# Block 0's first two feature rows as twenty-four parts by pair of heads, two tiles in a PSUM bank, with a new layout of the front stage

## The chip, the cores and the metric

The kernel runs on one core of a Trainium2 chip. The metric is the device time of one execution in microseconds (us), as the median of several runs.

## The reference

Three parts follow each other: an attention with a near and a far part, a dense layer with three candidates per hidden feature, and a layer of eight experts of which each token takes one. Only the first two matter here.

```python
# q, k, v: (4 batches, 8 heads, 576 positions, 64); factor 4
q_d = q.reshape(B, H, Sd, 4, D).mean(axis=3)        # k_d, v_d alike
far  = np.repeat(softmax(q_d @ k_d.T / 8) @ v_d, 4, axis=2)
mask = np.abs(pos[:, None] - pos[None, :]) < 4
near = softmax(np.where(mask, q @ k.T / 8, -1e9)) @ v
x = (far + near).transpose(0, 2, 1, 3).reshape(2304, 512)
h = np.maximum(np.maximum(x @ w1, x @ w2), x @ w3)  # (2304, 768)
x = h @ w_out                                       # (2304, 512)
# then: gate = argmax(x @ w_gate); out = p_gate * (relu(x @ w1[e]) @ w2[e])
```

## The kernel before, in words

**The attention's units.** The attention is cut into 16 units, one for each of the 4 batches and each of the 4 pairs of heads. Unit u is batch u // 4, pair u % 4. A unit loads its q and k transposed (tiles `qt`, `kt`) and its v (`vr`, `vb`), multiplies the near scores (`ts`, L408), takes maximum, exponential and sum (`smx`, `sm`, `sms`), turns the result on TensorE (`tt`) and multiplies it with v (`to`, L578); the far part does the same on rows summed by fours (`qk`, `td`, `dmx`, `ds`, `tu`, `tz`). At the end the two are added (`x`, L587), and x is split into a high half and a low half in the reduced fp32 format that TensorE takes (`xb`, L627 and L629). The low half is what the program calls `xl0` and `xl1`, one for each half of the positions.

**Forms.** The same piece can be done in several ways. The table `FORMS` gives each unit a set of two-letter flags: `pp` sums q and k by fours on TensorE (`tp`, L373) instead of VectorE; without `pb` and `px` the sum of far and near is made on VectorE; `pb` lets TensorE multiply the far part at full length (L564), `px` adds the far part on TensorE (L597); `nn` and `fn` put the normalisations on GpSimd; `nb`, `np` choose how the near maximum is subtracted, `np` on TensorE (L432).

**The weights.** w1, w2, w3 come as 64-bit floating-point words. Each of 18 pieces (6 columns blocks m times 3 matrices g) is loaded (`raw`, L816), its sign is cleared on ScalarE (L782), four VectorE operations of 128x512 narrow it to fp32 (L789, L791, L795, L799), ScalarE rounds it to a high half (`wh`, L804), and the low half `wl` is the rest: by a subtraction on VectorE or GpSimd (L807), or by two matmuls on TensorE (`wlow`, L843 and L844) with a copy behind them. The table `LOW` says which engine.

**The blocks.** x has 2304 rows (tokens), which are multiplied in nine blocks of 256. For each block 18 tiles of 128 features x 256 tokens are made, three (g = 0, 1, 2) for each of six **feature rows** m. A tile is 12 matmuls into one PSUM bank: four pairs of heads kk times three terms (high·high, high·low, low·high), all in `mul` (L1267), TensorE's row `hp<-xb,wh` and `hp<-xb,wl`. The three tiles of a feature row are reduced by a copy on ScalarE (`hid_first`, L1274) and two maxima on VectorE (`hid_max`, L1277), and later multiplied by w_out. There are four banks for this (`mm`).

**The order.** Nothing of this is placed by hand. A list scheduler, `Plan`, holds for each engine the time up to which it is filled. Each piece of work has an engine, an estimated duration, pieces that must come before it, buffers that it takes and gives back, and a due time `want`; the planner takes one after another and so fixes the order of instructions on each engine, including the order in which SyncE issues loads. The due times come from tables (`BATCH`, `PAIR`, `STEP`, `WEIGHTS`, `W_OUT`, `HIDDEN`, `ROWS`). Where TensorE would be idle by the plan for long, the planner puts in **fills**: matmuls of a constant that nobody reads (`warm`, L2401). On the chip each instruction waits for what it needs, in this fixed order.

Before, block j could begin when the low halves of **all** units of the batches it touches were done, `us = [4 * b + i ...]` in the last loop of the listing.

Of the kernel before, what the change touches and what calls it, by code (L numbers as in the profile page):

```python
# [19 lines left out]
B, H, S, D = 4, 8, 576, 64  # L20
# [11 lines left out]
TB = 256  # L32
# [18 lines left out]
FORMS = (  # L51
    "dv fn pb pp px sk sq",
    "nb nn np pb px sk sq",
    "dv fn nn np px sq xl xp",
    "pp sk xl",
    "nn pb px xl xp",
    "fn nn pp px sq xl",
    "nb px sq xl xp",
    "dv fn pp px xl xp",
    "dv nb np sk",  # L60
    "nb np sk xl",
    "dv nn sk sq xp",
    "nb sk",
    "nb np pp sq",
    "dv sk sq xp",
    "dv fn nn xl xp",
    "fn nb nn np sk xl xp",
)

LOW = (  # L70
    "DVE", "Pool", "DVE", "Pool", "DVE", "DVE",
    "PE", "Pool", "Pool", "Pool", "DVE", "Pool",
    "DVE", "DVE", "PE", "PE", "DVE", "DVE",
    "DVE", "Pool", "Pool", "DVE", "PE", "Pool",
)


BATCH, PAIR, STEP = (-278.0, 574.2, -146.8, 833.4), 90.18, (45.2, 112.5, 182.1, -110.2, -78.0, -138.8, 70.2, -165.1, -443.7, 7.1)
WEIGHTS, W_OUT = (-143.0, -97.3, 241.0, 361.9, 306.7, 570.1), (-2456.29, 74.04)
HIDDEN, ROWS, RESTS = (772.13, 191.47, -1093.51), (-324.96, -1170.55), 10.0  # L80

# [208 lines left out]
class Attention:  # L290
# [331 lines left out]
    def to_x(s, u, g, lo, on):  # L622
        xf = s.st[u]["x", g].rearrange("p a r -> p (a r)") if ("x", g) in s.st[u] else s.st[u]["to", g]
        for j, c, f, n in s.cut(u, g):
# [3 lines left out]
            else:  # L628
                s.on(on).tensor_tensor(out=w[:, 1], in0=xf[:, f:f + n], in1=w[:, 0].bitcast(F32), op=ALU.subtract)  # L629

    def plan(s, pl, u, want, flags):

        here, T = {}, STEP
# [5 lines left out]
        def add(name, eng, dur, fn, *after, t=0.0, get=(), put=(), act=None):  # L639
            after = [here[a] if isinstance(a, str) else a for a in after]  # L640
            port = eng == "Pool" or eng == "DVE" and name not in free and name not in ("sq", "sk")
            here[name] = pl.add(eng, dur, fn, after, want + t, get, put, act, port=port)
# [59 lines left out]
        if not one:  # L702
            add("of", "PE", 0.8, lambda: s.out_far(u), "cf", "sv", t=T[7], get=("at", "dn"), put=("pd", "vr"),
                act=0.54)
            add("cd", "ACT", 0.19, lambda: s.mean_far(u), "of", t=T[7], put=("at",))
        if one:
            for g in range(2):
# [3 lines left out]
                    act=1.09,  # L711
# [37 lines left out]
class Dense:  # L749
# [183 lines left out]
    def plan_block(s, pl, j, x, when):  # L933
# [8 lines left out]
        top, low, seven = {}, {}, j in SEVEN  # L942
        s.hid[j] = [None] * 6
        for n, m in enumerate((0, 1, 2, 4, 3, 5) if seven else range(6)):
            w = when(j) + n * 3
            for g in range(3):
                after = [pe, *x] if not m + g else [pe]
                after.append(s.jw[3 * m + g])

                def mul(m=m, g=g):  # L950
                    if m + g == 0:
                        first()
                    s.mul(j, m, g)

                pe = pl.add(
                    "PE", 1.37, mul, after, w, get=("mm",) if m + g else ("mm", s.ht_tag(j)),
                    put=("xb",) if m + g == 7 else (),
                )
                s.read[3 * m + g] = pe
                if g == 0:  # L960
                    b = pl.add("ACT", 0.27, lambda m=m: s.hid_first(j, m), [pe], w + HIDDEN[2], get=("hf",),
                        put=("mm",))
                else:
                    b = pl.add("DVE", 0.34, lambda m=m, g=g: s.hid_max(j, m, g), [pe, b], w + HIDDEN[2], put=("mm",), port=False)
            top[m], r = b, None
# [1406 lines left out]
def moe_kernel(ctx, tc, q, k, v, vs, w1, w2, w3, w_out, w_gate, e1, e2, cst, out):  # L2372
# [11 lines left out]
    with tc.manual_schedule():  # L2384
# [148 lines left out]
```

## Time and profile before

| what | value |
|---|---|
| median of 3 runs | 685.31 us (683.45 to 685.78) |
| the profiled execution: time, span, granted clock | 684.8 us, 683.0 us, 0.998 |
| TensorE busy (share of the span) | 667.1 us (98%) |
| VectorE busy | 432.0 us (63%) |
| ScalarE busy | 312.6 us |
| GpSimd busy | 127.0 us |
| first matmul of block 0 | 76.49 us after the span's start |

The span is the time from the first to the last instruction in the profile. The execution's own time is 1.8 us more than the span and 0.5 us below the median of the three runs. Busy time of TensorE counts the fills, which produce nothing. Busy shares are averages over stages that are limited by different things, so the stretch ahead of block 0 (the first 76.49 us) and the stretch behind it have to be read apart.

### The profile page before, as it was taken

What the parts mean: (1) busy time and instruction counts of PE and PEld (TensorE: products, weight loads), DVE (VectorE), ACT (ScalarE), POOL (GpSimd) and SP (SyncE); (2) the same over time, 40 slices, a digit from 0 to 9 for tenths busy, and PEclk for the clock granted to TensorE, in tenths of its full rate; (3) what the DMA queues carried; (4) which work ended last, traced back from release to release, by engine and by line L of the source; (5) the groups of instructions that cost most, each with busy time, mean ns of one, the idle gap of its engine ahead of it and who ended that gap; (6) DMA issues with size and microseconds to landing.
All of it is one profiled execution on the core that took longest, in us unless ns stands there. A gap on an engine that the chain in (4) does not pass through costs nothing.

```text
span 683.0 us, 16157 instructions
## 1 busy us (share of the span) xinstructions
PE 667.1 (98%) x6329; PEld 603.8 (88%) x6329; DVE 432.0 (63%) x1089; ACT 312.6 (46%) x904; POOL 127.0 (19%) x148
## 2 busy tenths in 40 slices
PE   8889999999999999999999999999999999999995
PEld 5566799989999999999999999998998989886775
DVE  5998986795544483225845558778653554597863
ACT  3765656676444353213322223441543443447753
POOL 2535432302401020101000000303211112101011
PEclk9999999999999999999999999999999999999999
DMA  7757524334422110101000005401617453463620
GB/s 250 236 171 233 193 69 117 117 92 149 127 76 59 57 40 1 50 1 49 1 32 1 33 1 182 173 33 32 189 48 241 138 174 102 138 208 126 231 83 31
DMA packets 32246, 73.18 MB, mean 107 GB/s; under 512 B 4319, under 2 KB 4575, under 8 KB 32160
## 3 DMA queue, kind: packets, MB, share of 16 engines
q1 hardware_dynamic: 26528, 57.63, 26.5%
q0 software_dynamic: 3040, 9.70, 4.3%
q10 hardware_dynamic: 2592, 4.72, 1.8%
q8 instruction: 52, 0.85, 0.5%
q14 instruction: 34, 0.28, 0.1%
HBM read 75.18 MB, written 9.70 MB: 124 GB/s over the span
## 4 chain that ended last, share of the span: by engine, by line
PE 88%; DVE 8%; DMA 1%; issue 1%; ACT 0%; SPq 0%; POOL 0%; POOLq 0%; DVEq 0%; ACTq 0%
PE hp L1267 32%; PE ehp L2043 11%; PE yp L1302 7%; PE eo L2015 7%; PE yp L1176 3%; PE ehp L2169 3%; PE eo L2210 3%; PE eo L2070 3%; PE racc L2332 2%; PE tp L373 2%; PE to L578 1%; PE ts L408 1%; PE xtp L2154 1%; PE tz L550 1%; PE tt L523 1%; PE td L489 1%
## 5 line engine op out<-in xcount | busy, mean ns | idle before, releaser
L1267 PE MATMUL hp<-xb,wh 128*128 128x256 f32 x1296 | 231.5, 282 | 0.3 <-issue 0.3
L1267 PEld LDWEIGHTS hp<-xb,wh 128*128 128x128 f32 x1296 | 196.4, 188 | 2.3 <-issue 1.4
L1267 PE MATMUL hp<-xb,wl 128*128 128x256 f32 x648 | 180.1, 278 | 0.0
L1267 PEld LDWEIGHTS hp<-xb,wl 128*128 128x128 f32 x648 | 121.9, 188 | 0.0
L1277 DVE TENSOR_TENSOR hf<-hf,hp 128x256 f32<-128x256 f32 x108 | 45.3, 420 | 74.9 <-PE hp L1267 73.3
L2043 PEld LDWEIGHTS ehp<-xT,ew 128*128 128x128 f32 x672 | 78.2, 188 | 4.2 <-issue 2.5
L2043 PE MATMUL ehp<-xT,ew 128*128 128x256 f32 x672 | 80.6, 279 | 0.0
L1284 ACT CAST ht<-hf 128x256 fp32r<-128x256 f32 (+1 forms) x54 | 21.1, 391 | 75.6 <-DVE hf L1277 75.3
L2139 POOL DMA_INDIRECT xg<-y,r_go x14 | 15.4, 1103 | 173.2 <-DMA eh<-in_moe_w_dram 112.0
L2227 POOL DMA_INDIRECT out_dram<-ob,r_si x17 | 17.2, 1014 | 117.7 <-ACT ob L2222 56.9
L1274 ACT COPY hf<-hp 128x256 f32<-128x256 f32 x54 | 20.2, 373 | 36.3 <-PE hp L1267 36.1
L2015 PE MATMUL eo<-eh,ehT 128*128 128x256 f32 x210 | 36.4, 280 | 0.0
L2015 PEld LDWEIGHTS eo<-eh,ehT 128*128 128x128 f32 x210 | 30.6, 188 | 2.5 <-issue 1.7
L2015 PE MATMUL eo<-el,ehT 128*128 128x256 f32 x130 | 31.4, 276 | 0.0
L2036 DVE SCALAR_TENSOR_TENSOR ob<-eo,r_ga,ob 128x256 f32<-128x256 f32 (+1 forms) x15 | 8.6, 571 | 32.4 <-PE eo L2015 31.6
L1966 ACT ACTIVATE ehT<-ehp 128x128 fp32r<-128x128 f32 (+1 forms) x40 | 13.3, 332 | 33.6 <-PE ehp L2043 32.7
L1288 DVE TENSOR_TENSOR ht<-hf,ht 128x256 fp32r<-128x256 f32 (+1 forms) x54 | 21.7, 402 | 10.0 <-ACT ht L1284 9.5
L1302 PE MATMUL yp<-wob,ht 128*128 128x264 f32 (+1 forms) x216 | 27.8, 284 | 0.0
L1302 PEld LDWEIGHTS yp<-wob,ht 128*128 128x128 f32 x216 | 26.7, 188 | 0.1
L1302 PE MATMUL yp<-woa,ht 128*128 128x256 f32 x216 | 26.1, 277 | 0.0
L1968 DVE SCALAR_TENSOR_TENSOR ehT<-ehp,ehT 128x128 fp32r<-128x128 f32 (+1 forms) x40 | 14.2, 354 | 18.4 <-ACT el L1951 16.5
L508 ACT ACTIVATE ds<-td,dmx 72x144 f32<-72x144 f32 x64 | 23.5, 376 | 4.9 <-DVE dmx L502 4.9
(333 smaller groups left out, 1389.5 us busy)
## 6 DMA issues: line engine op xcount, KB each, us to landing
rw<-in_moe_w_dram SPq DMA_DIRECT2D x64, 256.0 KB
eh<-in_moe_w_dram SPq DMA_DIRECT2D x20, 512.0 KB
el<-in_moe_w_dram SPq DMA_DIRECT2D x20, 512.0 KB
raw<-in_moe_w_dram SPq DMA_DIRECT2D x18, 512.0 KB
vb<-in_vs_dram SPq DMA_DIRECT2D x16, 320.0 KB
qt<-in_q_dram SPq DMA_DIRECT2D x16, 288.0 KB
kt<-in_k_dram SPq DMA_DIRECT2D x16, 288.0 KB
vr<-in_v_dram SPq DMA_DIRECT2D x16, 288.0 KB
```

What stands on the lines that cost most here:

```text
L508: s.nc.scalar.activation(out=st["ds"][:, a, :, h], in_=t[:, a].rearrange("p (k t) -> p t k", t=3), func=ACTF.Exp, bias=st["dm"][:, h, a:a ...
L1176: s.nc.tensor.matmul(s.yb[j, k][:, 0:n], h[x], r[y], start=first and i + p == 0, stop=i == 2 and p == 2, skip_group_check=True,)
L1267: s.nc.tensor.matmul(t, s.part(a, m, g)[:, kk], s.xb[j][:, x, kk], start=n == 0, stop=n == 11)
L1277: s.nc.vector.tensor_tensor(out=s.hf[j, m], in0=s.hf[j, m], in1=s.hp.pop((j, m, g)), op=ALU.max)
L1284: s.nc.scalar.copy(out=s.ht[j][:, 0, m, c], in_=s.hf[j, m][:, c])
L1288: s.nc.vector.tensor_tensor(out=s.first_low(j) if j in SEVEN and not m else h[:, 1, m, c], in0=s.hf[j, m][:, c], in1=h[:, 0, m, c].bitcast ...
L1302: s.nc.tensor.matmul(b[j, t, g], s.ht[j][:, int(i == 1), kk, ts], s.wo(int(i == 2), kk, g)[:, 0:n], start=q == 0, stop=q == 17)
L2015: s.nc.tensor.matmul(t, x[:, c:c + 128], y, start=m == 0 and first, stop=m == 11, skip_group_check=True,)
L2043: s.nc.tensor.matmul(t, s.W1[j][a][:, f * 128:(f + 1) * 128], s.xL[:, x, j], start=n == 0, stop=n == 11,)
L2070: s.nc.tensor.matmul(s.op[k, 0], h[a][:, j, i * 128:(i + 1) * 128], s.second(b, j), start=j == 0 and w == 0, stop=j == 7 and w == 2,)
L2169: s.nc.tensor.matmul(s.hp[k][f], a[:, j], s.W1[j][b][:, f * 512:(f + 1) * 512], start=j == 0 and w == 0, stop=j == 3 and w == 2,)
L2210: s.nc.tensor.matmul(s.op[k, cols.start], a[:, j], s.second(b, j, cols), start=j == 0 and w == 0, stop=j == 7 and w == 2)
```

## The change

Four things change together.

1. For block 0 the first six tiles (feature rows m = 0 and 1) are no longer made one after another. `plan_parts` makes 24 **parts** of three matmuls, ordered by pair of heads kk: six tiles for kk = 0, then six for kk = 1, and so on. A part waits for x of its own pair of heads and for its own weight. Two tiles share one bank of 2x256 columns, so the six hold three of the four banks from the first part until both tiles of a bank have been read; only the first matmul into a bank clears it. For kk = 3 the two tiles of a bank change places (`i ^= kk == 3`). For m = 1 the first copy is made by VectorE instead of ScalarE.
2. A block waits only for those low halves whose positions fall into it. For block 0 these are the first halves `xl0` of units 0 to 3.
3. The planner gets extra edges (`BEHIND`): the near and the far scores of unit u may be held back until the output multiplication `on` of unit u - v is placed.
4. All tables are new: the forms, the engine of each low half, one due time per unit instead of `BATCH` and `PAIR`, and the due times of weights and blocks.

```diff
 FORMS = (
-    "dv fn pb pp px sk sq",
+    "dv fn pp px sk sq xl",
...
 LOW = (
-    "DVE", "Pool", "DVE", "Pool", "DVE", "DVE",
+    "PE", "PE", "PE", "Pool", "Pool", "DVE",
...
+PARTS, PART = 6, 2219.9
...
-        add("n", "PE", 1.05, lambda: s.near(u), "lq", "lk", s.masked, get=("at", "at", "sm"), act=1.3)
+        add("n", "PE", 1.05, lambda: s.near(u), "lq", "lk", s.masked, s.behind(u, 0), get=("at", "at", "sm"), act=1.3)
...
+        parts, free = s.plan_parts(pl, x, when(j), first) if not j else [], []
...
-                pe = pl.add(
-                    "PE", 1.37, mul, after, w, get=("mm",) if m + g else ("mm", s.ht_tag(j)),
-                    put=("xb",) if m + g == 7 else (),
-                )
-                s.read[3 * m + g] = pe
+                if n * 3 + g < PARTS and not j:
+                    pe = parts[n * 3 + g & ~1]
...
+                e, d, x1 = ("ACT", 0.27, None) if put or not m else ("DVE", 0.34, free[-1])
...
+    def plan_parts(s, pl, x, w, first):
+
+        js, pe = {}, None
+        for kk in range(4):
+            for i in range(PARTS):
+                i ^= kk == 3
...
+                js[i] = pe = pl.add(
+                    "PE", 0.345, mul, [pe, x[kk], s.jw[i]], w + PART * kk,
+                    get=() if kk or i & 1 else ("mm",) if i else ("mm", "hT"),
+                )
+        return js
+
+    def mul_part(s, i, kk):
+        if not kk:
+            if not i & 1:
+                s.pair = s.bank(2 * TB, "hp")
+            s.hp[0, i // 3, i % 3] = s.pair[:, i % 2 * TB:i % 2 * TB + TB]
+        for n, (a, x) in enumerate(((0, 0), (0, 1), (1, 0))):
+            s.nc.tensor.matmul(
+                s.hp[0, i // 3, i % 3], s.part(a, i // 3, i % 3)[:, kk], s.xb[0][:, x, kk], start=not kk + i % 2 + n,
+                stop=kk == 3 and n == 2, skip_group_check=True,
+            )
...
-            us = [4 * b + i for b in {j * TB // S, (j * TB + TB - 1) // S} for i in range(4)]
-            x = [at.jobs[u][f"xl{g}"] for u in us for g in range(2)]
+            x = [at.jobs[u][f"xl{g}"] for u in range(at.n) for g in range(2) if j in [c[0] for c in at.cut(u, g)]]
```

**The opening, on SyncE's queue.** SyncE issues the loads: constants `cs`, gate weights `wg`, the mask `pt`, q and k of the first unit, its v (`vr`), and the 64-bit weights `raw`. Before, the program begins so:

```order
L2390 DMA cs<-in_consts_dram 128x130
L908 DMA wg<-in_moe_w_gate_dram 128x4x8
L316 DMA pt<-in_consts_dram 128x192
L334 DMA qt<-in_q_dram 128x576
L334 DMA kt<-in_k_dram 128x576
L342 DMA vr<-in_v_dram 96x768
L816 DMA raw<-in_moe_w_dram 128x1024
```

The changed program begins so (the lines are about ten to fifty higher):

```order
L2443 DMA cs<-in_consts_dram 128x130
L829 DMA raw<-in_moe_w_dram 128x1024 x3
L921 DMA wg<-in_moe_w_gate_dram 128x4x8
L351 DMA vr<-in_v_dram 96x768
L325 DMA pt<-in_consts_dram 128x192
L343 DMA qt<-in_q_dram 128x576
L829 DMA raw<-in_moe_w_dram 128x1024
L343 DMA kt<-in_k_dram 128x576
```

Three weights of 512 KB each, and v, now stand ahead of q, and a fourth weight stands ahead of k. There are three `raw` buffers.

**Ahead of block 0, on TensorE's queue.** Before, all of the twelve matmuls of a tile stand together behind the attention (here the end of the first tile, `hp_1029`, and the beginning of the second, `hp_1047`; two rows are one kk):

```order
L1267 MATMUL hp_1029<-xb_70,wh_72 128x256 x2
L1267 MATMUL hp_1029<-xb_70,wl_81 128x256
L1267 MATMUL hp_1029<-xb_70,wh_72 128x256 x2
L1267 MATMUL hp_1029<-xb_70,wl_81 128x256
L1267 MATMUL hp_1047<-xb_70,wh_72 128x256 x2
L1267 MATMUL hp_1047<-xb_70,wl_81 128x256
```

Everything of batch 0's attention stands ahead of these rows. In the changed program the parts stand between the attention's pieces. These rows are the end of the parts of kk = 2 (`hp_640` and `hp_738` are the second and third bank), with the turning of the near result `tt` and the far output `tz` of the last unit of batch 0 between them:

```order
L1026 MATMUL hp_640<-xb_70,wh_73 128x256 x2
L1026 MATMUL hp_640<-xb_70,wl_82 128x256
L532 MATMUL tt_980<-cs_66,sm_819 128x128 x3
L1026 MATMUL hp_640<-xb_70,wh_73 128x256 x2
L1026 MATMUL hp_640<-xb_70,wl_82 128x256
L1026 MATMUL hp_738<-xb_70,wh_74 128x256 x2
L1026 MATMUL hp_738<-xb_70,wl_83 128x256
L1026 MATMUL hp_738<-xb_70,wh_74 128x256 x2
L1026 MATMUL hp_738<-xb_70,wl_83 128x256
L559 MATMUL tz_998<-pd_891,vr_900 128x144 x3
```

Eighteen parts have moved ahead of that `tz`; behind it come four fills, the rest of the turning, the near scores of a later unit, and then the six parts of kk = 3.

**Around the last rows of x, on VectorE's queue.** Before (the rows of 128x512 are narrowing operations of weights; `x<-to,dn` makes the last x rows of batch 0, and their split into halves is ScalarE's and GpSimd's):

```order
L467 TENSOR_SCALAR sms<-sms 128x10
L502 TENSOR_SCALAR dmx<-dmx 72x4
L795 SCALAR_TENSOR_TENSOR tmp<-raw,tmp 128x512
L471 RECIPROCAL sms<-sms 128x10
L799 SCALAR_TENSOR_TENSOR tmp<-raw,tmp 128x512
L789 TENSOR_SCALAR tmp<-tmp 128x512
L587 TENSOR_TENSOR x<-to,dn 128x288 x2
```

Changed:

```order
L820 TENSOR_TENSOR wl<-tmp,wh 128x512
L812 SCALAR_TENSOR_TENSOR tmp<-raw,tmp 128x512
L802 TENSOR_SCALAR tmp<-tmp 128x512
L804 TENSOR_SCALAR tmp<-tmp 128x512
L808 SCALAR_TENSOR_TENSOR tmp<-raw,tmp 128x512
L596 TENSOR_TENSOR x<-to,dn 128x288 x2
L812 SCALAR_TENSOR_TENSOR tmp<-raw,tmp 128x512
L638 TENSOR_TENSOR xb<-x,xb 128x256
```

The last low half `xb<-x,xb` has come to VectorE. Ahead of the last `x` stood 53 narrowing operations; now 71 stand ahead of `x`, and 72, the whole of the 18 pieces, ahead of that last low half.

## Rows read from the trace of the kernel before

**Rows 1.** The page, chain that ended last, by engine (shares of the span).

```profile
PE 88%; DVE 8%; DMA 1%; issue 1%; ACT 0%; SPq 0%; POOL 0%; POOLq 0%; DVEq 0%; ACTq 0%
```

**Rows 2.** Busy time of each engine in three stretches (us from the span's start).

```profile
core 0: us, PE busy (x) PEld busy (x) DVE busy (x) ACT busy (x) POOL busy (x), PEclk, DMA share, GB/s
0.00:76.49 76.49, 68.88 (x717) 44.81 (x717) 64.23 (x146) 44.38 (x140) 35.34 (x37) 1.00 0.67 220
76.49:660.00 583.51, 582.81 (x5526) 545.42 (x5520) 360.05 (x936) 261.34 (x757) 88.68 (x109) 1.00 0.29 94
660.00:683.00 23.00, 15.45 (x95) 13.57 (x93) 7.72 (x9) 6.85 (x9) 2.94 (x3) 0.93 0.19 71
```

**Rows 3.** TensorE's fills ahead of block 0, grouped by line.

```profile
L2401 PE MATMUL warm<-const-bfloat16-1.0 128*128 128x512 bf16 x85 | 22.6, 404 | 0.8 <-PEq L2520 0.8
```

**Rows 4.** What TensorE waited for, 0 to 80 us; the longest wait.

```profile
PE tt L523 <- DVE tmp L789: 2.0, 1, 2.0
```

**Rows 5.** TensorE's timeline at block 0's start: start, length, line, operation.

```profile
73.65 1.91 PE L2401 MATMUL warm<-const-bfloat16-1.0 128*128 128x512 bf16 x8
...
76.49 0.51 PE L1267 MATMUL hp<-xb,wh 128*128 128x256 f32 x2
...
76.95 0.39 PE L1267 MATMUL hp<-xb,wh 128*128 128x256 f32 x2
...
77.29 0.39 PE L1267 MATMUL hp<-xb,wh 128*128 128x256 f32 x2
```

**Rows 6.** VectorE's timeline: a weight's operations, and the last x rows.

```profile
61.83 1.48 DVE L795 SCALAR_TENSOR_TENSOR tmp<-raw,tmp 128x512 int32<-128x512 int32 x1
...
67.74 0.68 DVE L795 SCALAR_TENSOR_TENSOR tmp<-raw,tmp 128x512 int32<-128x512 int32 x1
68.34 0.42 DVE L789 TENSOR_SCALAR tmp<-tmp 128x512 f32<-128x512 f32 x1
68.68 0.68 DVE L799 SCALAR_TENSOR_TENSOR tmp<-raw,tmp 128x512 int32<-128x512 int32 x1
...
72.49 0.81 DVE L587 TENSOR_TENSOR x<-to,dn 128x288 f32<-128x288 f32 x2
```

**Rows 7.** TensorE's timeline, 38 to 54 us: the attention's pieces.

```profile
38.12 1.35 PE L432 MATMUL ts<-smx,nid 128*128 128x320 f32 x4
39.30 3.08 PE L564 MATMUL to<-pd,vr 96*128 96x288 f32 x12
42.31 0.81 PE L578 MATMUL to<-pt,vb 64*64 64x58 f32 x40
...
45.27 1.02 PE L843 MATMUL wlow<-tmp,cs 128*128 128x512 f32 x2
...
46.37 0.38 PE L523 MATMUL tt<-cs,sm 128*128 128x128 f32 x2
...
47.40 2.20 PE L373 MATMUL tp<-qt,cs 128*128 128x144 f32 x8
49.43 0.92 PE L550 MATMUL tz<-pd,vr 96*128 96x144 f32 x6
50.18 0.19 PE L399 MATMUL ts<-mask,ident 128*128 128x64 bf16 x1
...
53.75 1.15 PE L597 MATMUL to<-dn,cs 128*128 128x288 f32 x4
```

**Rows 8.** All engines' timeline, the opening.

```profile
2.66 0.30 ACT L306 CAST ident<-cs 128x128 bf16<-128x128 f32 x1 [0.62 <-DMA cs<-in_consts_dram]
...
3.64 0.42 SPq L816 DMA_DIRECT2D raw<-in_moe_w_dram  x1
...
6.94 0.79 PE L408 MATMUL ts<-kt,qt 64*58 64x64 f32 x40 [1.10 <-DMA kt<-in_k_dram]
...
8.06 0.55 DVE L384 TENSOR_TENSOR vr<-vr 96x384 f32<-96x384 f32 x1 [8.06 <-DMA vr<-in_v_dram]
...
9.42 0.67 ACT L782 ACTIVATE tmp<-raw 128x512 f32<-128x512 f32 x1 [4.49 <-DMA raw<-in_moe_w_dram]
```

More of the change, by code (lines that the diff above doesn't have):

```diff
@@ L51 @@
 FORMS = (
[L52 to L67 removed]
+    "dv fn pp px sk sq xl",
+    "fn nb nn pb xl xp",
+    "nn np px sk sq",
+    "dv fn np pp sk",
+    "fn px xl",
+    "dv pp px xl",
+    "px sq xl",
+    "dv fn nn np pp sq xl",
+    "dv nn np sk sq xl xp",
+    "fn nn xp",
+    "dv fn nn sk sq xl",
+    "dv nb np sk sq xl xp",
+    "dv sq xp",
+    "dv fn nn sk xl",
+    "fn nb np xl",
+    "dv nn xp",
 )
 LOW = (
[L71 to L80 removed]
+    "PE", "PE", "PE", "Pool", "Pool", "DVE",
+    "PE", "DVE", "Pool", "DVE", "DVE", "PE",
+    "DVE", "PE", "DVE", "DVE", "Pool", "Pool",
+    "Pool", "Pool", "DVE", "PE", "PE", "DVE",
+)
+PARTS, PART = 6, 2219.9
+UNITS = (
+    -3483.9, -758.8, -4540.4, -2253.4, 7756.1, 1783.0, 5057.9, -4418.9,
+    -4751.3, -3370.6, 1669.8, -4780.8, 1801.9, -2432.5, -4741.3, 2312.0,
+)
+STEP = (8763.6, 220.3, 11431.0, 1051.8, -5522.3, -5513.1, 3554.9, -2205.7, 9163.7, 1400.4)
+BEHIND = (
+    (0, 0, 0, 0, 0, 3, 3, 2, 0, 3, 0, 3, 2, 2, 3, 2),
+    (0, 0, 0, 0, 1, 2, 3, 3, 0, 4, 1, 4, 1, 0, 3, 2),
+)
+WEIGHTS, W_OUT = (-2155.4, 3788.5, -12510.7, -1045.1, 5542.9, 8860.7), (-9153.9, -13064.7)
+HIDDEN, ROWS, RESTS = (9646.6, 8551.4, -18442.7), (3612.3, -7279.7), 10.0
 BUSY, HALF = 0.6, 1.7
@@ L629, in to_x, with behind @@
                 s.on(on).tensor_tensor(out=w[:, 1], in0=xf[:, f:f + n], in1=w[:, 0].bitcast(F32), op=ALU.subtract)
+    def behind(s, u, i):
+        v = BEHIND[i][u]
+        return s.jobs[u - v]["on"] if v else None
     def plan(s, pl, u, want, flags):
@@ L639, in add @@
         def add(name, eng, dur, fn, *after, t=0.0, get=(), put=(), act=None):
-            after = [here[a] if isinstance(a, str) else a for a in after]
+            after = [here[a] if isinstance(a, str) else a for a in after if a]
             port = eng == "Pool" or eng == "DVE" and name not in free and name not in ("sq", "sk")
@@ L678, in plan @@
         either("nn", 0.74, 1.36, lambda e: s.near_norm(u, e), "ni", t=T[3])
-        add("f", "PE", 0.65, lambda: s.far(u), "sk", t=T[4], get=("at", "at", "ds"), put=("qk",), act=0.5)
+        add("f", "PE", 0.65, lambda: s.far(u), "sk", s.behind(u, 1), t=T[4], get=("at", "at", "ds"), put=("qk",), act=0.5)
         for h in range(2):
@@ L953, in mul @@
                     s.mul(j, m, g)
-                pe = pl.add(
-                    "PE", 1.37, mul, after, w, get=("mm",) if m + g else ("mm", s.ht_tag(j)),
-                    put=("xb",) if m + g == 7 else (),
-                )
-                s.read[3 * m + g] = pe
+                if n * 3 + g < PARTS and not j:
+                    pe = parts[n * 3 + g & ~1]
+                else:
+                    pe = pl.add(
+                        "PE", 1.37, mul, after, w, get=("mm",) if m + g else ("mm", s.ht_tag(j)),
+                        put=("xb",) if m + g == 7 else (),
+                    )
+                s.read[3 * m + g], put = pe, () if n * 3 + g < PARTS and not j else ("mm",)
+                e, d, x1 = ("ACT", 0.27, None) if put or not m else ("DVE", 0.34, free[-1])
                 if g == 0:
-                    b = pl.add("ACT", 0.27, lambda m=m: s.hid_first(j, m), [pe], w + HIDDEN[2], get=("hf",),
-                        put=("mm",))
-                else:
-                    b = pl.add("DVE", 0.34, lambda m=m, g=g: s.hid_max(j, m, g), [pe, b], w + HIDDEN[2], put=("mm",), port=False)
+                    b = pl.add(
+                        e, d, lambda m=m, e=e: s.hid_first(j, m, e), [pe, x1], w + HIDDEN[2], get=("hf",), put=put, port=False,
+                    )
+                else:
+                    b = pl.add(
+                        "DVE", 0.34, lambda m=m, g=g: s.hid_max(j, m, g), [pe, b], w + HIDDEN[2], put=put, port=False,
+                    )
+                free.append(b)
+                if not put and 3 * n + g & 1:
+                    pl.add("PE", 0, lambda: None, free[-1:], w + HIDDEN[2], put=("mm",))
             top[m], r = b, None
@@ L1270, in mul, with hid_first @@
                 n += 1
-    def hid_first(s, j, m):
+    def hid_first(s, j, m, on):
         s.hf[j, m] = s.pool.tile([128, TB], F32, name="hf", tag="hf", bufs=2)
-        s.nc.scalar.copy(out=s.hf[j, m], in_=s.hp.pop((j, m, 0)))
+        (s.nc.scalar.copy if on == "ACT" else s.nc.vector.tensor_copy)(out=s.hf[j, m], in_=s.hp.pop((j, m, 0)))
     def hid_max(s, j, m, g):
@@ L2414, in moe_kernel @@
         for u in range(at.n):
-            at.plan(pl, u, BATCH[u // 4] + PAIR * (u % 4), FORMS[u].split())
+            at.plan(pl, u, UNITS[u], FORMS[u].split())
         dn.plan_w(pl, lambda i: WEIGHTS[i // 3] + i % 3 / 2)
```

6 lines of the change are left out of this document (added).

## The prediction

> **What bounds the kernel now.** I read first the chain that ended last: 88% of it is TensorE [rows 1]. Then the windows: from the first matmul of block 0 at 76.49 us to 660 us TensorE is busy 582.81 of 583.51 us at full granted clock [rows 2]. So behind 76.49 nothing but the amount of TensorE's work sets the time. The stretch ahead of it is different. There TensorE shows 68.88 us busy of 76.49, but 22.6 us of that are 85 fills that produce nothing [rows 2, 3], whereas VectorE works 64.23 us though its first operation starts at 8.06 [rows 2, 8]: only 68.43 - 64.23 = 4.2 us idle from then on. Block 0 can't start before the last x rows, which VectorE makes at 72.49 [rows 6]; TensorE spends the 1.91 us from 73.65 on fills and begins at 76.49 [rows 5]. **VectorE's list bounds the opening stretch, TensorE's work the rest.** The change is therefore worth: how much useful TensorE work is done by the moment T at which the last input of block 0 is there, and how that moment moves. The time changes by (T - 76.49) minus the extra work done ahead of T plus the change in TensorE's whole work.
>
> **What TensorE's whole work becomes.** Prices are distances between starts [rows 7]; counts are from the two programs. Full-length far products, `to<-pd,vr`: two units fewer at 42.31 - 39.30 = 3.01, -6.0. Sums by fours, `tp`: one unit's q and k fewer at 2.03 each, -4.1. Low halves of x by TensorE: gone, twelve matmuls, about -1.3 by their widths (estimate from the 1.15 us of four wider ones at 53.75). Far part `tz`: two more at 0.75, +1.5. Adding the far part: one more at about 1.1. Subtracting the near maximum: three pairs more at 1.18, +3.5. Low halves of weights: three more at 46.37 - 45.27 = 1.10, +3.3, and one of w_out, +1.1. Sum: **-0.9**. Fills don't count here: all stand ahead of T, before and now.
>
> **What is done ahead of T.** Of parts, 18 of 24 stand ahead of the last unit's end; a part is 77.29 - 76.95 = 0.34 us [rows 5], 6.1. Of the rest of TensorE's order up to there: four low halves of weights more, +4.4; one near subtraction more, +1.2; one `tz`, +0.75; one far addition, +1.1; one full-length product fewer, -3.0; one far score `td` fewer, -0.65 (estimate between its neighbours' 0.75 and 0.4). Sum: **+9.9 us** of work that lay behind 76.49 or replaces what lay there. TensorE has room: ahead of T it has by this list 56.3 us of work, and 54 fills (the program holds 31 fewer than before) of 1.91 / 8 = 0.24 us [rows 5], 13 us: about 70 in all.
>
> **When T is.** VectorE lists, ahead of the last low half of block 0 (its own now, in place of ScalarE's and GpSimd's split), 72 narrowing operations where 53 stood ahead of the last x. Two of a weight's four cost 0.34, two 0.60 [rows 6]; the 19 more are ten long and nine short, 10 x 0.60 + 9 x 0.34 = 9.1. The other differences (the last x and its half, one more low half and normalisation; two far maxima, two far normalisations and two near subtractions fewer) lie between 0.3 and 0.8 each and nearly cancel: +0.2. So VectorE has 9.3 us more to do. Some of the present operations last longer than that, such as the 1.48 at 61.83 against 0.68 for the same operation at 67.74 [rows 6]; over the stretch VectorE's list, 54 us at the short prices, took 72.49 - 8.06 - 4.2 = 60.2, a factor of 1.11. So the 9.3 are 9.3 to 10.4. Against that VectorE starts earlier: its first work was v's, landed at 8.06; now it is a weight's, and three weights are issued right behind the constants. A weight issued at 3.64 was on ScalarE at 9.42 [rows 8]. Issued 2.4 us earlier it is there by 7.0 at the latest; at the earliest, 2.3 us (512 KB at the stretch's 220 GB/s [rows 2]) behind the constants' 2.66, at 5.0. With ScalarE's 0.67 ahead of it VectorE starts between 5.7 and 7.7; I take 6.4, near the early end as nothing but 65 KB is ahead on the queue: -1.7. T = 72.49 + 9.3 - 1.7 = 80.1 at the short prices, 81.2 at the long ones; **I take 80.6**.
>
> **The sum.** 80.6 - 76.49 = +4.1; -9.9; -0.9: **-6.7**, from 684.8 to 678.1 of the profiled execution. The runs' median is 0.5 above that one, so 678.6 for the median.
>
> **Edits that I cost at nothing.** The second copy on VectorE (m = 1) adds one operation of some 0.4 behind T, where VectorE is busy 360 of 583 us [rows 2]; without that cover a bank would come free 0.4 later. The three held banks leave one for other tiles and low halves until T; the attention has tiles of its own, so what can wait is a low half of a weight, of which the last is listed ahead of the parts of kk = 2. The shorter list of rows that a block waits for would matter only where TensorE waits for x, and behind 76.49 it waited 0.7 us in all [rows 2]. The new hold-backs `BEHIND` only shape the order.
>
> **Rivals.** *Full gain* (0.12): VectorE's 4.2 us of waits vanish too, as weights now stand between the attention's operations; T is 76, TensorE's 70 still fit, and the time is 678.6 - 4.6 = 674. *Given back later* (0.16): the attention of batches 1 to 3 has new forms and due times, and its pieces stand between tiles; that TensorE waited 0.7 us in 583 was a property of the old layout. Waits of 2 to 4 us there, half of the 76.49 - 68.88 = 7.6 us that TensorE was idle in the opening, give 680.6 to 682.6. *No change* (0.11): pieces of attention in the opening wait for each other, VectorE included, as TensorE did for 2.0 us for one VectorE operation [rows 4]; four such waits more put T to 87 or 88 and eat the gain: 684.5 to 686. *Late opening, slower* (0.08): k of the first unit is now behind 2 MB of weights, and the fourth weight must wait for a buffer, so for the narrowing of the first one, some 1.9 us after VectorE's start. Ahead of k's end lie 3.1 MB, at 220 GB/s 14 us; I expect the first near score at 13 instead of 6.94 [rows 8]. In my forecast that is covered: VectorE has 16 narrowing operations, v's sums and a low half listed ahead of its first near maximum, 9.6 us from 6.4 on, until 16. But if the attention's own chain, 72.49 - 6.94 = 65.6 us long, sets the pace and VectorE's added work falls into it, T is 13 + 65.6 + 9.3 = 88; break-even is 76.49 + 9.9 + 0.9 = 87.3, and it is measurably slower from 89.4 on; at 90, 688. *Clock* (0.03): fills kept TensorE active, and 31 of them go. Its granted clock stood at 1.00, the 2.4 GHz level, in the whole opening, through its longest gap of 2.0 us at that; only in the tail, where TensorE is busy 15.45 of 23 us, is the mean 0.93 [rows 2, 4]. At the 1.2 GHz level a stretch of work lasts twice as long; TensorE has some 10 us to spare ahead of T, so it costs nothing until more than 10 us of its work run so, and the whole gain when 17 do: about 685.
>
> The Trainium skill ("TensorE: Matmul & The Clock Gate", Part 1, "HAM oscillation — how this bites in real kernels") warns that idle gaps between bursts of matmuls bring the half clock back each time. By that rule the removed fills are a loss; the trace so far doesn't bear it out, since the gap of 2.0 us passed without a drop. I leave it at the 0.03 above.
>
> **How the numbers follow.** The forecast holds with 0.50, its own range 676.5 to 681 (T from 78.5 to 83, by VectorE's start and the stretching). With the rivals: below 676.5 0.12, 681 to 683.2 0.16, no change 0.14 with the clock, slower 0.08. About 0.3%, or 2.1 us, is what a measurement of this kernel tells from no change. Faster is the forecast, the full gain and what is given back: 0.78. I move 0.01 of it and 0.01 of no change to slower, for bank or buffer waits that I didn't see: faster 0.77, same 0.13, slower 0.10. The range from 675.0 to 684.8 leaves out part of the full gain (0.06) and the worse half of the last two (0.13).
>
> **What the profile would show.** The parts of kk = 3 begin near 80.6, those of kk = 0 long before; TensorE's matmuls up to there include 18 parts and 54 fills; VectorE starts near 6.4 and is hardly idle until the last low half; behind the parts TensorE's idle time stays under 1 us. The prediction is wrong if T is above 85, if gaps of several us appear behind it, if the granted clock falls below 1.00 in the opening, or if VectorE waits for near scores at 16 us.

## The result, and the profile after

The changed kernel takes **675.56 us** (median of 4 runs, 675.28 to 675.66), the kernel before beside it 685.54 us (median of 4, 683.45 to 688.36): ratio 0.985, 95% interval [0.982, 0.989]. It is faster by 10 us, where 678.6 and a gain of 6.7 had been forecast. The profiled execution takes 675.66 us, its span is 673.8, so against the profiled execution of before (684.8) it is 9.1 us faster; the rest of the 10 is mainly that one's place, 0.7 below its median.

The last pair's first part is issued by TensorE at 78.94 us. The windows of the changed kernel, cut there (columns as in [rows 2]):

```profile
core 0: us, PE busy (x) PEld busy (x) DVE busy (x) ACT busy (x) POOL busy (x), PEclk, DMA share, GB/s
0.00:78.94 78.94, 73.99 (x743) 51.03 (x746) 70.54 (x155) 49.45 (x144) 20.65 (x26) 0.98 0.70 227
78.94:650.80 571.86, 571.46 (x5453) 535.15 (x5447) 362.44 (x934) 246.81 (x672) 94.20 (x120) 1.00 0.29 94
650.80:673.80 23.00, 16.39 (x99) 14.34 (x98) 8.65 (x10) 6.82 (x9) 2.93 (x3) 0.94 0.22 77
```

Behind the cut TensorE is busy 571.46 of 571.86 us: nothing was given back there. So the reading of before holds: the time is the moment T plus what is left. Before, 683.0 - 76.49 = 606.5 us were left; now 673.8 - 78.94 = 594.9. The fills ahead of block 0, grouped by line, answer [rows 3]:

```profile
L2454 PE MATMUL warm<-const-bfloat16-1.0 128*128 128x512 bf16 x51 | 14.8, 436 | 1.1 <-PEq L2572 0.8 <-DVE tmp L812 0.2
```

The profile holds 51 of the 54 that the program lists there. TensorE's timeline at block 0 answers [rows 5]; the first two rows are the end of kk = 2, the row at 77.99 shows TensorE's last wait ahead of T (the number in brackets is idle time, and what ended it), the row at 78.94 is the first part of kk = 3, the last row the first whole tile:

```profile
74.61 0.39 PE L1026 MATMUL hp<-xb,wh 128*128 128x256 f32 x2
74.84 0.28 PE L1026 MATMUL hp<-xb,wl 128*128 128x256 f32 x1
74.96 0.90 PE L559 MATMUL tz<-pd,vr 96*128 96x144 f32 x6
...
77.99 0.19 PE L408 MATMUL ts<-mask,ident 128*128 128x64 bf16 x1 [0.56 <-DVE x L596]
...
78.22 0.79 PE L417 MATMUL ts<-kt,qt 64*58 64x64 f32 x40
78.94 0.74 PE L1026 MATMUL hp<-xb,wh 128*128 128x256 f32 x2
...
82.19 0.40 PE L1320 MATMUL hp<-xb,wh 128*128 128x256 f32 x2
```

VectorE's timeline around the last x, and the opening on all engines, answer [rows 6] and [rows 8]:

```profile
75.86 1.71 DVE L808 SCALAR_TENSOR_TENSOR tmp<-raw,tmp 128x512 int32<-128x512 int32 x1
77.49 0.81 DVE L596 TENSOR_TENSOR x<-to,dn 128x288 f32<-128x288 f32 x2
...
78.83 0.95 DVE L638 TENSOR_TENSOR xb<-x,xb 128x256 fp32r<-128x256 f32 x4
```

```profile
4.96 0.66 ACT L795 ACTIVATE tmp<-raw 128x512 f32<-128x512 f32 x1 [1.73 <-DMA raw<-in_moe_w_dram]
...
5.66 0.43 DVE L802 TENSOR_SCALAR tmp<-tmp 128x512 f32<-128x512 f32 x1 [5.66 <-ACT tmp L795]
...
13.16 0.65 PEld L417 LDWEIGHTS ts<-kt,qt 64*58 64x58 f32 x40 [1.27 <-DMA kt<-in_k_dram]
```

What VectorE waited for up to 90 us (line, what it waited for: us in all, times, longest):

```profile
DVE tmp L802 <- ACT tmp L795: 5.7, 1, 5.7
DVE dmx L507 <- PE td L498: 1.8, 2, 1.6
```

VectorE starts at 5.66 instead of 8.06 and delivers the last x at 77.49. From its start to T it is idle 78.94 - 5.66 - 70.54 = 2.7 us instead of 4.2; the 1.8 us of `dmx` are the waits among them that are long enough to be listed. The first near score comes at 13.16 instead of 6.94, as the changed order of loads suggested.

### The profile page after: what moved, and what is told of

Same layout as the page of the kernel before. It is cut to its first block, busy times and chain, and to the rows that moved or that the text cites. A ratio compares the mean times of both kernels' runs of the same rounds, so it can differ in the third digit from the quotient of the medians.

```text
span 673.8 us, 16007 instructions
## 1 busy us (share of the span) xinstructions
PE 661.8 (98%) x6286; PEld 600.5 (89%) x6289; DVE 441.6 (66%) x1097; ACT 303.1 (45%) x824; POOL 117.8 (17%) x149
## 4 chain that ended last, share of the span: by engine, by line
PE 92%; DVE 4%; DMA 2%; issue 1%; POOL 0%; POOLq 0%; ACT 0%; SPq 0%; DVEq 0%
PE hp L1320 32%; PE ehp L2096 12%; PE yp L1355 8%; PE eo L2068 7%; PE yp L1229 3%; PE ehp L2222 3%; PE eo L2263 3%; PE eo L2123 3%; PE racc L2385 2%; PE ts L417 2%; PE tz L559 2%; PE td L498 1%; PE to L587 1%; PE tp L382 1%; PE xtp L2207 1%; DMA raw<-in_moe_w_dram 1%
## 5 line engine op out<-in xcount | busy, mean ns | idle before, releaser
L1320 PE MATMUL hp<-xb,wh 128*128 128x256 f32 x1248 | 220.3, 280 | 0.4 <-issue 0.4
L1320 PEld LDWEIGHTS hp<-xb,wh 128*128 128x128 f32 x1248 | 188.9, 188 | 2.0 <-issue 1.2
L1320 PE MATMUL hp<-xb,wl 128*128 128x256 f32 x624 | 173.2, 278 | 0.0
L1320 PEld LDWEIGHTS hp<-xb,wl 128*128 128x128 f32 x624 | 117.5, 188 | 0.0
L2096 PE MATMUL ehp<-xT,ew 128*128 128x256 f32 x672 | 80.6, 279 | 0.0
L1337 ACT CAST ht<-hf 128x256 fp32r<-128x256 f32 (+1 forms) x54 | 21.0, 389 | 80.6 <-DVE hf L1330 77.7
L1355 PE MATMUL yp<-wob,ht 128*128 128x264 f32 (+1 forms) x216 | 29.9, 288 | 0.0
L1355 PE MATMUL yp<-woa,ht 128*128 128x256 f32 x216 | 27.5, 282 | 0.0
L1355 PEld LDWEIGHTS yp<-woa,ht 128*128 128x128 f32 x216 | 25.8, 188 | 0.7 <-issue 0.6
```

Of the source, the lines that this page charges most:

```text
L1320: s.nc.tensor.matmul(t, s.part(a, m, g)[:, kk], s.xb[j][:, x, kk], start=n == 0, stop=n == 11)
L1337: s.nc.scalar.copy(out=s.ht[j][:, 0, m, c], in_=s.hf[j, m][:, c])
L1355: s.nc.tensor.matmul(b[j, t, g], s.ht[j][:, int(i == 1), kk, ts], s.wo(int(i == 2), kk, g)[:, 0:n], start=q == 0, stop=q == 17)
L2096: s.nc.tensor.matmul(t, s.W1[j][a][:, f * 128:(f + 1) * 128], s.xL[:, x, j], start=n == 0, stop=n == 11,)
```

## The experiments

In all of them T is the start of the first part of kk = 3 on TensorE; where the early parts are issued late, it is the start of the first of them, which then stand directly ahead of those of kk = 3. The first weight landed at different times in these executions, so that VectorE began between 5.54 and 6.31 us in the profiles with the new opening. A difference of some tenths between two T tells nothing by itself.

**The parts issued late.** All else in its order:

```diff
+        js, pe, late = {}, None, []
...
-                    s.mul_part(i, kk)
+                    late.append((i, kk))
+                    for a in late if kk == 3 else ():
+                        s.mul_part(*a)
+                    if kk == 3:
+                        late.clear()
```

> The changed kernel with nothing moved but this: the 18 parts of the first three pairs of heads are issued only when the last pair's parts are, directly ahead of them; order of all else, fills and tables as in the changed kernel. My theory (the opening is set by VectorE's list, the rest by the amount of TensorE's work left): the parts' first matmul of the last pair's data still becomes possible near 79 us, and 18 x 0.34 = 6.1 us of work now lie behind it, so 681.7 us, 6.1 above the changed kernel's 675.6. Rival (the parts only took the place of fills, the gain is that of the new tables): within 1 us of 675.6. Rival (the opening is set by TensorE's queue): the moment comes earlier as the parts leave the queue, 675.6 to 678.

Measured: 681.39 us (10 runs), ratio to the kernel before 0.994 [0.993, 0.996]; 5.8 more than the changed kernel. All 24 parts now begin where six did:

```profile
78.39 0.50 PE L1030 MATMUL hp<-xb,wh 128*128 128x256 f32 x2
```

So inside the new layout the parts are worth 5.8 us, nearly their whole length of 6.1; the layout without early parts is 4.3 us faster than the kernel before beside it (685.7). That the parts left TensorE's queue moved the moment by 0.55 us only (78.39), and TensorE now stood idle where they had been; the two longest of these waits behind 60 us are for ScalarE's results:

```profile
PE to L606 <- ACT dn L563: 1.5, 1, 1.5
...
PE tz L559 <- ACT pt L540: 1.1, 1, 1.1
```

**The parts alone, in the kernel before.** Its tables and order stay; parts go into TensorE's queue where the plan says that x and weight are there:

```diff
+            for j in order:
...
+                while parts and j["eng"] == "PE" and j["dur"]:
+                    i, kk = parts[0]
+                    d = [at.jobs[kk]["xl0"], dn.jw[i]]
+                    if not all(id(x) in done and done[id(x)] + 0.4 < j["start"] for x in d):
+                        break
+                    part()
```

> The kernel before with its own tables and its own order, and only the first two feature rows of block 0 made as 24 parts, 18 of them issued where x of their pair and their weight are there by the plan, in place of fills (two fills fewer for each part, 36 fewer in all). My theory: VectorE still delivers the last x at 72.5 and block 0's last pair begins near 76.5, so 6.1 us of work are done ahead of it: 679.4, 6.1 below the kernel before. Rival (parts alone are worth nothing without the new layout, since they wait for x or weights in the queue and push the attention back): 684 to 687. Rival (parts in the queue delay the attention somewhat): 680.5 to 683.

Measured: 687.26 us (10 runs), ratio 1.001 [0.999, 1.003]: no gain at all. T is 81.45 instead of 76.49 in the profile, whose execution is the slowest of the ten (691.4). Its windows show the granted clock falling to a mean of 0.83 and 0.66:

```profile
60.00:70.00 10.00, 6.83 (x75) 6.25 (x76) 8.51 (x17) 4.21 (x12) 3.81 (x5) 0.83 0.46 141
70.00:80.00 10.00, 7.76 (x65) 5.56 (x64) 6.93 (x16) 5.10 (x17) 3.30 (x3) 0.66 0.66 216
```

That left open whether the clock or the layout took the gain, so the same was run with all fills kept.

> As the run with the parts alone in the kernel before, but with all of that kernel's fills left in their places. There 36 fills were taken out; TensorE's granted clock fell to 0.66 in the ten microseconds from 70 us and block 0's last pair began at 81.4 instead of 76.5. If that loss came from the clock after TensorE's gaps (theory now), the clock stays at 1.00 here, the last pair begins between 78 and 80, since the queue has 6.1 us more ahead of it and 7.6 us of idle time, and the time is 685.7 - 6.1 + 2 to 4 = 681.6 to 683.6. Rival (parts in the old layout wait for x or a weight in the queue and hold the attention up, clock or not): the last pair begins at 81 or later, 684.5 to 687.

Measured: 690.74 us (4 runs), ratio 1.009 [1.007, 1.011]. The clock stood at 0.85 from 20 to 30 us and at 1.00 from 30 to 80, and T still was 80.39: just short of the rival's 81, and the time lies beyond the rival's 687. So a low clock is not what took the gain; the rival's mechanism, the attention held up, fits, as VectorE now waits 3.8 us for near scores (first row) where it waited 1.6 (second row, the kernel before). Then the windows cut at T, and the longest wait of TensorE from 80 to 110 us:

```profile
DVE smx L418 <- PE ts L408: 3.8, 2, 2.4
...
DVE smx L418 <- PE ts L408: 1.6, 1, 1.6
```

```profile
0.00:80.39 80.39, 75.78 (x726) 51.39 (x727) 62.56 (x145) 44.32 (x138) 33.21 (x36) 0.98 0.63 208
80.39:650.00 569.61, 564.39 (x5436) 529.25 (x5435) 347.59 (x923) 250.30 (x744) 89.28 (x110) 1.00 0.30 95
```

```profile
PE wlow L843 <- DVE tmp L799: 4.0, 1, 4.0
```

T moved by 3.9 us. Behind T TensorE was idle 5.2 us instead of 0.7, of which 4.0 are one wait for a weight's narrowing, which VectorE does late in that layout, and the mean clock from 80 to 100 us was 0.89 and 0.94. Against 6.1 us of work done ahead that is a loss. So in the old layout the parts gain nothing, with the fills or without. What in the new layout they need, the weights or the attention, no run separates.

**More work on VectorE.**

```diff
-            s.narrow(st["w"][1], st["v"], i)
+            for _ in range(8 if eighth and i == 0 else 1):
+                s.narrow(st["w"][1], st["v"], i)
```

> The changed kernel in its own order, with the first narrowing operation of the ninth weight issued eight times instead of once on VectorE (it clamps, so that repeating it changes nothing): seven more operations of 0.34 us, 2.4 us, well ahead of the last x. My theory (VectorE sets the moment at which block 0's last inputs are there): the last pair's parts begin 2.4 us later, the time is 675.6 + 2.4 = 678.0. Rival (the attention's own chain, or TensorE's queue, sets it and VectorE's list has room): 675.6 to 676.4.

Measured: 679.95 us (5 runs), ratio 0.992 [0.989, 0.995], 4.4 more than the changed kernel; T 83.45, so 4.5 later for 2.4 us of work by the estimate. The eight operations on VectorE and two later ones (at 25.39 and 77.49 in the changed kernel), then TensorE's longest wait, for a later weight's narrowing, and the window from 20 us, in which the mean granted clock was 0.54:

```profile
10.10 3.65 DVE L802 TENSOR_SCALAR tmp<-tmp 128x512 f32<-128x512 f32 x8
...
29.03 0.68 DVE L812 SCALAR_TENSOR_TENSOR tmp<-raw,tmp 128x512 int32<-128x512 int32 x1
...
82.00 0.81 DVE L596 TENSOR_TENSOR x<-to,dn 128x288 f32<-128x288 f32 x2
```

```profile
21.47 2.05 PE L858 MATMUL wlow<-tmp,cs 128*128 128x512 f32 x2 [3.33 <-DVE tmp L812]
```

```profile
20.00:30.00 10.00, 7.88 (x58) 4.05 (x58) 9.90 (x23) 5.51 (x15) 0.05 (x1) 0.54 0.76 262
```

TensorE's pieces there last twice as long (2.05 for two matmuls that took 1.02 in [rows 7]). But little of the 4.5 us is the clock's, as VectorE's operations show when they are laid beside those of the changed kernel. Its first began 0.65 later (6.31 for 5.66), which has nothing to do with the edit. The seven more took 3.0: each works on what the one before has just written, and they follow each other at 3.65 / 8 = 0.46 us and not at 0.34. That makes 3.65, and from 13 to 29 us every operation runs that much later (29.03 for 25.39), through most of the stretch of low clock. Only 0.9 came behind it, at VectorE's waits for TensorE's scores near 30 and 38 us. From 38 us to T every operation of VectorE is 4.5 us late (82.00 for 77.49), and TensorE's first part with it. VectorE's list is on the path.

**More work on TensorE.** Two fills more in each later group: `n += 2 * (3 < len(calls) < 11)`.

> The changed kernel in its own order, with two fills more in each of the seven later groups of fills ahead of block 0: 14 x 0.22 = 3.0 us more in TensorE's queue, which produce nothing. My theory (VectorE's list sets the moment, TensorE has slack, ten microseconds by my list): 675.6, within 0.7. Rival (TensorE's queue, or the pieces that wait for TensorE in it, sets it): 677.5 to 678.6.

Measured: 677.09 us (4 runs), ratio 0.988 [0.986, 0.990]; T 80.67. That is 1.7 us for 3.0 us of fills. Neither the theory (675.6, within 0.7) nor the rival (677.5 or more) gave it: TensorE's queue has not ten microseconds of slack where it matters.

**No fills** but the first six.

> The changed kernel in its own order, without the fills ahead of block 0 but for the first six: 48 fewer, 28 of them ahead of the first near scores. Theory (fills do nothing but keep the granted clock up): the clock is at its lower level, 0.50, wherever TensorE has just had gaps, so in most of the first 50 us; the pieces of attention there last up to twice as long, VectorE waits for them, and the last pair begins 3 to 10 us later: 678 to 686. Rival (TensorE's slack covers a slow opening): 675.6, within 1. Rival (fills only cost queue time): 674 to 675.

Measured: 676.22 us (4 runs), ratio 0.987 [0.985, 0.989]; T 79.83. The mean clock was 0.86 from 20 to 30 us, 0.97 from 30 to 40 and 0.92 and 0.91 from 70 to 90, not low in most of the opening. By the medians the 48 fills are worth 0.7 us here (1.3 by the two ratios), not told apart from nothing by these runs.

**The old opening**, the mask and the first unit's q and k loaded ahead of the weights:

```diff
+        pl.jobs[0]["fn"]()
+        for c in "qk":
+            at.load_t(0, c)
```

> The changed kernel with the loads of the mask and of the first unit's q and k issued right behind the constants, as before the change, ahead of the three weights; all else in its order. The weights land 672 KB later, 1.7 to 2.5 us, the first near scores some 6 us earlier. My theory (VectorE's start sets the moment): VectorE starts at 7.5 to 8.2 instead of 5.7, the time is 2 us more, 677 to 678. Rival (the late near scores cost time, the attention's chain sets the moment): 670 to 675. Rival (neither, gaps elsewhere take it up): within 0.7 of 675.6.

Measured: 677.84 us (4 runs), ratio 0.990 [0.988, 0.992]; T 80.65.

```profile
8.16 0.43 DVE L806 TENSOR_SCALAR tmp<-tmp 128x512 f32<-128x512 f32 x1 [8.16 <-ACT tmp L799]
...
12.40 0.79 PE L421 MATMUL ts<-kt,qt 64*58 64x64 f32 x40
```

VectorE started 2.5 us later, T came 1.7 later. The first near score is hardly earlier (12.40), since TensorE's queue holds the fills and a weight's low half ahead of it; so this run tests VectorE's start and not the late near score.

**Less work on VectorE ahead of T.** The narrowing of late weights goes behind the last x. In a first build those operations on these weights that stood behind the last x stayed in their old place, ahead of the narrowing that they need, so that it computed other values; its 755.83 us tell nothing here, its expectation was much that of the next run. With all that depends on the narrowing behind it:

```diff
...
-        for j in pl.run():
+        for j in later(pl.run(), at.jobs[3]["xl0"], dn.cleared[15:]):
```

> The changed kernel with the narrowing of the last three of 18 weights taken from ahead of the last x on VectorE's queue and put one by one between the operations behind it, everything that depends on it behind it: 13 VectorE operations, 6.2 us at the short prices, leave the stretch ahead of block 0's last input. These weights are read by the last three tiles of the block, 14 us later. My theory (VectorE's list sets that moment): it comes 3 to 6.2 us earlier, 669.5 to 673 us. Rival (the attention's chain sets it, VectorE's narrowing only fills the gaps): within 0.7 us of 675.6. Rival (given back: VectorE reads the tiles late, banks come free late and TensorE waits): 675 to 678, with waits of TensorE of several us just behind the parts.

Measured: 683.03 us (7 runs), ratio 0.996 [0.995, 0.998]; 7.5 slower than the changed kernel. T came 0.5 earlier (78.40) and not 3 to 6: VectorE, with nothing left to do, waited 5.3 us for the last unit's far part, which ScalarE takes from TensorE's `tz`. That `tz` stands where TensorE's list reaches it, and TensorE didn't pause (first row, a window):

```profile
70.00:76.00 6.00, 6.00 (x76) 5.23 (x75) 1.14 (x3) 1.75 (x4) 0.00 (x0) 1.00 0.46 147
...
70.65 0.55 DVE L395 TENSOR_TENSOR vr<-vr,cs 96x384 f32<-96x384 f32 x1
76.53 0.82 DVE L596 TENSOR_TENSOR x<-to,dn 128x288 f32<-128x288 f32 x2 [5.33 <-ACT dn L563]
```

Behind T the third possibility happened, TensorE waited for VectorE to free banks and for the next near part; from 90 to 100 us the mean clock was 0.83:

```profile
PE hp L1322 <- DVE hf L1332: 2.3, 1, 2.3
...
PE td L498 <- DVE sm L433: 1.3, 1, 1.3
```

> The same with the last weight alone: four or five VectorE operations, some 2 us, leave the stretch. My theory: 1 to 2 us earlier, 673.6 to 674.6, a third of what three weights give. Rival (attention's chain): 675.6, within 0.7.

Measured: 676.21 us (5 runs), ratio 0.987 [0.985, 0.989], the rival's time; T 78.20, with 1.1 us of wait for VectorE behind it.

**Both lists shorter at once.**

> Both reliefs at once, in the changed kernel: its 18 early parts issued late (6.1 us out of TensorE's queue ahead of the last pair; alone the first late part began at 78.4 instead of 78.9) and the narrowing of the last three weights behind the last x (6.2 us out of VectorE's list; alone 78.4). Theory now (two lists of nearly the same length, each covers for the other when one alone is shortened): the moment comes several us earlier, 73 to 76. Rival (the attention's own chain of dependent pieces is that long, whatever else stands in the queues): 77.5 or later. The time is not better either way, since 6.1 us of work move behind the moment and VectorE reads the tiles late: about 685.

Measured: 685.85 us (9 runs), ratio 1.000 [0.999, 1.002]. The first late part:

```profile
78.09 0.50 PE L1032 MATMUL hp<-xb,wh 128*128 128x256 f32 x2
```

T is 78.09, as the rival had it, and VectorE waits for the far part here too:

```profile
76.22 0.82 DVE L596 TENSOR_TENSOR x<-to,dn 128x288 f32<-128x288 f32 x2 [4.59 <-ACT dn L563]
```

But this doesn't decide for the rival. TensorE waited 1.53 us for `dn` up to 64.59, and behind that the clock was at its lower level, 0.50, up to about 67.9. The same two pieces, first in this run with a window, then in the run with the parts late:

```profile
64.59 2.29 PE L606 MATMUL to<-dn,cs 128*128 128x288 f32 x4 [1.53 <-ACT dn L563]
66.81 1.28 PE L587 MATMUL to<-pt,vb 64*64 64x58 f32 x40
65.00:66.00 1.00, 1.00 (x3) 0.71 (x3) 1.00 (x4) 0.52 (x1) 0.00 (x0) 0.50 0.88 299
...
64.41 1.24 PE L606 MATMUL to<-dn,cs 128*128 128x288 f32 x4 [1.53 <-ACT dn L563]
65.58 0.81 PE L587 MATMUL to<-pt,vb 64*64 64x58 f32 x40
```

From the first start to the next piece it is 3.43 us here (to 68.02) and 1.90 there (to 66.31). Without these 1.5 us T would be about 76.6, an estimate that takes all of it through to T: between the theory's 76 and the rival's 77.5. And from 64.59 to T TensorE was idle 0.6 of 13.5 us, so what VectorE waits for there is TensorE's list, in which the last unit's `tz` stands behind other pieces.

**One weight, placed further behind.** As with one weight, but the moved operations begin eight VectorE operations later.

> The changed kernel with the last weight's narrowing behind the last x, as in the run with one weight, but only behind the next unit's near maximum and subtraction and the first tiles' maxima, so that TensorE no longer waits for those (1.1 us there). Theory: the last pair begins at 78.2 as in that run, nothing is lost behind it, 674.8 to 675.0, 0.7 below the changed kernel. Rival (the 0.7 are lost again to another wait behind it): 675.6 or more.

Measured: 676.78 us (6 runs), ratio 0.987 [0.985, 0.989], again the rival's side; T is 78.82 in its profile, in which VectorE began at 6.16 (5.54 in that of the run with one weight), and behind T TensorE waited 1.2 us for ScalarE's `ds` instead. No run beat the changed kernel.

## Why the prediction was right

The measured 675.56 lies below the forecast's own range (676.5 to 681), in the stretch that I had given to the full gain with 0.12; it is inside the whole range that I gave (675.0 to 684.8). Both halves of the sum erred to the same side, T by 1.7 us and what is left behind it by 0.85, so nothing cancelled by luck.

**The form of the sum held.** T plus what is left gives every run that only changes the opening: 673.8 - 78.94 = 594.9, and 678.2 - 83.45 = 594.8, 675.9 - 80.67 = 595.2, 675.0 - 79.83 = 595.2, 675.7 - 80.65 = 595.1 with more VectorE work, more fills, none, and the old opening.

**Work ahead of T and work in all, -9.9 and -0.9.** The rest behind T fell by 11.65 where 10.8 were forecast. TensorE's busy time behind T fell by 10.4 (582.81 + 15.45 against 571.46 + 16.39). The two terms are seen only in this sum, not one by one. The missing 0.85 is no work: from the start of the last VectorE operation to the span's end it was 7.51 us in the profile of before and 6.57 in that of after, and 6.6 to 7.6 over all runs here but the first build of late weights. Measured to that last operation (675.49 and 667.23) the change is -8.26; the forecast's -10.8 with the measured T gives 2.45 - 10.8 = -8.35.

**The moment T was mis-sized: 80.6 forecast, 78.94 measured.** Two terms of it were off, both to the long side. VectorE's start: I took 6.4 of a range from 5.7 to 7.7, and it was 5.66; the first weight was on ScalarE at 4.96, right at the early bound. And I kept VectorE's 4.2 us of idle time of before, which shrank to 2.7. Together that is 2.2 us. VectorE's work itself was right: 60.2 + 9.8 = 70.0 us were forecast, and from 5.66 to the last low half at 78.83 it was busy 70.4, long operations included, as the 1.71 us at 75.86 for one that took 0.68 in [rows 6]. The rival of the full gain had said that the waits go altogether (T 76); T went about a third of the way from 80.6 towards it.

**What sets T was only half right.** I held VectorE's list to be the bound and TensorE to have ten microseconds of room. The first holds in the changed kernel: with VectorE's list made longer or begun later, T follows. The second doesn't: ahead of T TensorE was busy 73.99 us where my list said about 70, and its room lies in the wrong place. By the windows (every row ten microseconds but the last, of six) it is in the first thirty microseconds; from 30 us on TensorE is full, up to its last wait of 0.56 us at 77.99:

```profile
20.00:30.00 10.00, 8.43 (x72) 5.34 (x74) 9.96 (x26) 7.96 (x25) 1.61 (x3) 0.83 0.83 271
30.00:40.00 10.00, 9.96 (x96) 6.72 (x95) 9.78 (x24) 7.85 (x35) 4.70 (x7) 1.00 0.65 219
...
60.00:70.00 10.00, 9.96 (x132) 8.24 (x132) 9.96 (x25) 6.49 (x16) 1.83 (x3) 1.00 0.84 266
70.00:76.00 6.00, 5.94 (x74) 5.01 (x73) 5.86 (x13) 2.79 (x7) 0.24 (x1) 1.00 0.38 131
```

So two lists end within about half a microsecond of each other, and each covers for the other: shortening VectorE's by 6.2 us moved T by 0.5, with TensorE full; shortening TensorE's by 6.1 moved it by 0.55, with VectorE full; 3.0 us of fills on TensorE's moved it by 1.7. Both shortened together moved it by 0.85, and the clock may have taken up to 1.5 us more of what that gave. Whether a third bound, such as a chain of dependent pieces of the attention, stands close behind the two lists, these runs don't settle; whether an earlier first near score alone would bring T forward was not tried, as the one run that loaded q and k first still had them behind TensorE's fills.

**The rivals.** *Given back later* did not happen (0.4 us idle behind T). *Late opening* did not decide: the first near score came at 13.16, as estimated, but VectorE took up the near maximum at 17.61 only, after its weights. *No change* by pieces that wait for each other did not come in the changed kernel, but it is much like what the parts did in the old layout, where they gave nothing. *Clock*: the rows below are the changed kernel's microseconds from 19 to 27, with the mean granted clock behind the busy times.

```profile
19.00:20.00 1.00, 0.30 (x2) 0.00 (x0) 0.97 (x3) 0.69 (x2) 0.00 (x0) 1.00 0.77 295
20.00:21.00 1.00, 0.06 (x1) 0.06 (x1) 0.96 (x3) 0.89 (x3) 0.00 (x0) 1.00 1.00 381
...
22.00:23.00 1.00, 0.81 (x3) 0.46 (x3) 1.00 (x6) 0.84 (x2) 0.00 (x0) 0.82 0.04 14
23.00:24.00 1.00, 1.00 (x2) 0.12 (x1) 1.00 (x2) 0.83 (x2) 0.00 (x0) 0.50 0.74 193
...
25.00:26.00 1.00, 1.00 (x40) 0.88 (x36) 1.00 (x5) 0.82 (x5) 0.00 (x0) 0.50 1.05 383
26.00:27.00 1.00, 0.83 (x9) 0.67 (x7) 1.00 (x4) 1.00 (x6) 0.00 (x0) 0.97 0.95 326
```

After TensorE had been busy 0.36 of two microseconds, waiting 1.64 us for ScalarE, the clock was at its lower level, 0.50 or 1.2 GHz, from about 22.6 to 26. I had named a clock below 1.00 in the opening as a sign of being wrong, and given it a chance of 0.03, on the ground that a gap of 2.0 us passed without it in [rows 4]. That ground was thin. The Trainium skill ("TensorE: Matmul & The Clock Gate", Part 1, "HAM oscillation — how this bites in real kernels") warns that gaps between bursts bring the half clock. This stretch agrees; the last two runs don't, where a wait of 1.78 us in the same place passed at 1.00. It cost little, some 0.3 us by one comparison: in the profile of the last run VectorE's operations ran 0.3 us behind those of the changed kernel ahead of that stretch and level with them behind 34 us.

## What to carry to other kernels

Cut the span at the moment from which one engine never idles again, and account for two numbers apart: when that moment comes, and how much of that engine's work is done by then. Fills are a sign of room for real work, but work put in their place pays only if its inputs are there that early; the same parts gave 5.8 us in one layout and nothing in another. That an engine's list fills a stretch does not make it the only bound: shorten it before believing it, since a second list of nearly the same length can stand right behind. And before an effect is put down to the clock, lay the engine's operations of the two traces side by side: where the delay arises, operation by operation, tells its cause.

## What the runs showed of the hardware

VectorE operations of 128x512 that each work on what the one before has just written followed each other at 0.46 us (eight in 3.65), others of the kind at 0.34 [rows 6]. Behind a wait of 3.3 us on TensorE the mean granted clock was 0.54 from 20 to 30 us, and two matmuls took 2.05 us instead of 1.02; of VectorE's delay of 4.5 us in that run 0.9 arose behind it. Removing 48 fills cost 0.7 us by the medians. In two other builds whose first 20 us hold the same instructions the clock stayed at 1.00 from 20 to 30 us where the changed kernel's profile shows 0.83: gaps of much the same length (1.64 us, and 1.78 in the two) bring the lower clock in one execution and not in another. The kernel before shows it too: in the executions of it beside the experiments the mean granted clock lies between 0.989 and 0.998; those with 0.998, like the profiled one, take 684.0 to 685.5 us, those with 0.992 or less 686.7 to 689.4.
